# Six PSUM banks for the last weight-gradient products, two for the rows beside them

## The chip, the core and the metric

One kernel runs on one core of a Trainium2 chip. The metric is the device time of one execution in microseconds. The execution that the profiler recorded has a span of its own, from its first to its last recorded instruction, and a device time a little longer than that span.

## The reference, cut to what matters

A forward pass of two residual blocks and its full gradient. `x` is 2048 x 448; block A multiplies its two-dimensional spectrum by learned weights, block B is an MLP over the 2048 tokens (hidden size F = 1792).

```python
h   = x + irfft2(rfft2(layernorm(x)) * (w_r + 1j * w_i))
h2  = h + mlp(layernorm(h))                 # w1: 2048x1792, w2: 1792x2048, gelu between
out, vjp = jax.vjp(h2_of, x, w_r, w_i, w1, b1, w2, b2)
return out, *vjp(grad_out)                  # out_0 .. out_7
```

The end of the kernel makes three of the outputs. `out_6` is the gradient of `w2` (1792 x 2048) and `out_4` that of `w1` (2048 x 1792): products of two 2-D operands contracted over the 448 columns. `out_1` is the gradient of `x`: rows of an inverse transform, put through the backward of a layer norm.

## The kernel before, in words

All work of TensorE, VectorE, ScalarE and of SyncE's queue stands in the order in which the program emits it; GpSimd's order alone is left to the scheduler.

PSUM has eight banks. `ps_ff()` (L177) and `ps_mm()` (L180) each hand out tiles of 128 x 512 fp32, one bank each, from two rings of four.

**Background products.** `gw_gen` (L1279) is a generator that yields once per unit of work. It runs over `u`, pairs of 128-row blocks of a weight gradient, and over four column blocks `c` of up to 512 columns. The contraction of 448 is three whole steps of 128 and one of 64. For the two row blocks of a pair, the two 64-row steps sit in one stationary tile (rows 0 to 63 for `i = 0`, 64 to 127 for `i = 1`); `parts` issues them as a pair of 64-row matmuls into two banks. A column block is thus six whole matmuls (`whole`), one pair of 64-row matmuls (`parts`), and two copies out of PSUM (`out`, through `evac`). The generator takes column blocks two at a time: six wholes of the first, then one visit of 64-row matmuls for both, then the copies of the first and the six wholes of the second. That is 14 units (`yield`) for two column blocks, 7 each.

Two such generators are queued in `pending`: one for `out_6` (7 pairs `u`, 196 units), then one for `out_4` (8 pairs, 224 units, its last column block of each `u` 256 wide). `fill(n)` takes n units from them, and after each unit pops one entry of `row_ops`. `evac` (L190) gives a copy to ScalarE or VectorE by the running totals of `Meter`, a cost table in the program. `store` and `st_load` issue the stores and the transposed loads of later stationary tiles on SyncE.

**The inverse rows.** After `s2_stage` (L687), whose last round uses the four `ff` banks for the last time in that form, `inv_rows` (L751) walks 16 row tiles. With two `aT` buffers it runs one tile ahead. Tile t of the loop is, in order of the program: `first(t+1)` (four 128-column matmuls into an `ff` bank, copied to `rAT` by ScalarE), `fill(8)`, then `py` (four 224-column matmuls into the two halves of another `ff` bank), then `gx_consumer`.

`gx_consumer` (L1346) puts the row's work into `row_ops`, to be popped during the next tile's `fill(8)`:

- `scaled_sum`: ScalarE reads the lower half of `py`, with a row sum;
- `low` and `high`: VectorE reads the upper half of `py` twice, once forwards and once reversed; after `high` the bank is free;
- `products`: a VectorE product with a row sum, and two GpSimd operations on single columns;
- `line`, `add_line`, `finish`: three VectorE operations in SBUF, held back for two tiles.

Before the change the order popped is `scaled_sum`, `low`, `line`, `high`, `add_line`, `products`, `finish`, where `line`, `add_line` and `finish` are those of two tiles earlier. After the 16 tiles, `drain()` runs what is left of `pending`.

Units, counted from the loops: `rows` and the fill after it take 54, `s2_stage` takes 33 in each of five rounds, 13 of them ahead of its second group of small matmuls and 20 at the round's end. When the last round's `after` hook is reached, 199 units are gone: all 196 of the first generator and three wholes of the second. 44 more are taken before `inv_rows`, 128 in it, and 49 in `drain()`.

Of the kernel before, what the change touches and what calls it, by code (L numbers as in the profile page):

```python
# [11 lines left out]
F32 = mybir.dt.float32  # L12
# [5 lines left out]
P = 128  # L18
# [23 lines left out]
N_FILL_B = (16, 16, 30, 8, 24, 8)  # L42
# [61 lines left out]
class Ring:  # L104
# [7 lines left out]
    def next(self):  # L112
        v = self.views[self.i % len(self.views)]
        self.i += 1
        Ring.release(v)
        return v
# [8 lines left out]
def kernel(  # L125
# [32 lines left out]
    psum = ctx.enter_context(tc.tile_pool(name="psum", bufs=1, space=bass.MemoryType.PSUM))  # L158
# [15 lines left out]
        n = int(np.prod(dims))  # L174
        return Ring([cut(reg, off + i * n, *dims) for i in range(count)])

    def ps_ff(parts=P):  # L177
        return psum.tile([P, 512], F32, tag="ff", bufs=4, name="ps_ff")

    def ps_mm():  # L180
        return psum.tile([P, 512], F32, tag="mm", bufs=4, name="ps_mm")


    def evac(out, in_, scale=None):
        n = int(np.prod(in_.shape[1:]))
        if load[0] + sc.cost('copy', n, False) <= load[1] + ve.cost('tensor_copy', n, in_.dtype == BF16):
            if scale is None:
                sc.copy(out=out, in_=in_)
            else:
                sc.activation(out=out, in_=in_, func=ACT.Copy, scale=scale)  # L190
        elif scale is None:
            ve.tensor_copy(out=out, in_=in_)
        else:
            ve.tensor_scalar(out=out, in0=in_, scalar1=scale, scalar2=None, op0=ALU.mult)
# [9 lines left out]
    def defer(us, fn, *views):  # L204
        state = [fn]

        def run():
            if state:
                state.pop()()
        later.append((clock[0] + us, len(later), run))  # L210
        later.sort(key=lambda x: x[0])
        for v in views:
            Ring.held.setdefault(id(v), []).append(run)
# [5 lines left out]
    def mm(out, lhsT, rhs, start, stop):  # L219
        nc.tensor.matmul(out, lhsT=lhsT, rhs=rhs, start=start, stop=stop)  # L220
        clock[0] += int(np.prod(rhs.shape[1:])) / 2400.0
        run_due()
# [373 lines left out]
    X_ring = ring(rC, 0, 2, 4, 2, KW)  # L596
# [189 lines left out]
    pending, row_ops = [], []  # L786

    def fill(n):
        while n > 0 and pending:
            try:  # L790
                next(pending[0])
                n -= 1
                if row_ops:
                    row_ops.pop(0)()
            except StopIteration:
                pending.pop(0)
# [101 lines left out]
    for c in range(2):  # L898
        for e in range(2):
            sc.copy(out=Rp.rearrange("p (e a q b c) -> p c e a q b", e=2, c=2, q=8, a=2)[:, c, e],  # L900
                    in_=Rm[:, 64 * c + 32 * e:64 * c + 32 * e + 32].rearrange("p (q a b) -> p a q b", q=8, a=2))
# [161 lines left out]
    for jp in range(NFB // 2):  # L1063
# [7 lines left out]
        for jj, ta, tb in spans:  # L1071
            fb = f0 + jj
            pu = pus[jj]
            for t in range(ta, tb):
                mm(pu[:, 0:D], lhsT=w1c[:, t, jj * P:(jj + 1) * P], rhs=hln[:, t, :],
                                 start=(t == 0), stop=(t == NT - 1))
# [136 lines left out]
    def load_du(q):  # L1213
        n = du_t[q].shape[1] * 512
        nc.sync.dma_start_transpose(out=du_t[q].rearrange("p j b q -> p (j b) q"), in_=rD[:, 2048 * q:2048 * q + n])
# [8 lines left out]
    st_next = iter(st_at)  # L1224

    def st_load(n):
        if n < 15:
            reg, j = order[n]
            nc.sync.dma_start_transpose(out=st_at[n], in_=reg[:, j * 1024 + 64:j * 1024 + 960])
# [3 lines left out]
    def load_xall(q):  # L1233
        nc.sync.dma_start(out=xall[:, 4 * q:4 * q + 4, :], in_=x_pt[:, 4 * q:4 * q + 4, :])
# [38 lines left out]
    ost = ring(rO, 0, 6, S // 2)  # L1273
    o4 = out_4.rearrange("(p t) f -> p t f", t=NT)

    def gw_gen(n, rhs, width, store, ost, u0=0):
        for u in range(u0, u0 + n // 2):
            st = next(st_next)

            def whole(pw, w, c, i, k, start, stop):  # L1280
                mm(pw[i][:, 0:w], lhsT=st[:, 4 * i + k, :], rhs=rhs(c, k, 0, P), start=start, stop=stop)

            def parts(pw, w, c, start):
                for i in range(2):
                    mm(pw[i][:, 0:w], lhsT=st[64 * i:64 * i + 64, 3, :], rhs=rhs(c, 3, 64 * i, 64 * i + 64),
                       start=start, stop=not start)

            def out(pw, w, c, i):
                o = os_[i]
                x = c % 2 * 512  # L1290
                evac(out=o[:, x:x + w], in_=pw[i][:, 0:w])
                if x:
                    if c == 3 and i and u != 3:
                        st_load(u + 4 if u < 3 else u + 3)
                    defer(1.5, lambda j=2 * (u - u0) + i: store(j, 512 * (c - 1), x + w, o), o)

            for c in range(0, 4, 2):
                os_ = [ost.next(), ost.next()]
                pw = [ps_mm(), ps_mm()]
                for i in range(2):  # L1300
                    for k in range(3):
                        whole(pw, 512, c, i, k, k == 0, False)
                        yield
                w = min(512, width - 512 * (c + 1))
                pv = [ps_mm(), ps_mm()]
                parts(pw, 512, c, False)
                parts(pv, w, c + 1, True)
                for i in range(2):
                    out(pw, 512, c, i)
                yield  # L1310
                yield
                for i in range(2):
                    for k in range(3):
                        whole(pv, w, c + 1, i, k, False, k == 2)
                        if k == 2:
                            out(pv, w, c + 1, i)
                        yield

    def store_4(t, a, n, o):
# [8 lines left out]
    for t in range(NT - LAG, NT + 4):  # L1328
        if t == 13:
            st_load(3)  # L1330
        if t == NT - 2:
            fill(8)
        rows(t)
    fill(N_FILL_B[2])
    Meter.slack = 7.0
    s2_stage(lambda s: X_ring.next(), bwd_mult, 13, 20, N_FILL_B[4], {0: lambda: load_du(1), 1: lambda: (load_du(0), load_xall(0)), 2: lambda: load_xall(1), 3: lambda: load_du(2)},
             2.0 * INV_SD)
    Meter.slack = 2.0
    g_out = w_io(out_2, out_3, True)
# [3 lines left out]
    def gx_consumer(t, py):  # L1343
        if t in X_AT:
            load_xall(X_AT[t])
        for _ in range(GW_AT.count(t)):  # L1346
            next(g_out, None)
        pb, tmp = (r448[:, t % 8 * D:(t % 8 + 1) * D], r452[:, t % 8 * D:(t % 8 + 1) * D])
        ms, m1, m2 = (lcol[:, NT + t, k:k + 1] for k in range(3))
        u, s2, s1 = (gcol[:, t, k:k + 1] for k in range(3))  # L1350
        nmean, rstd2, md = (xcol[:, k, t:t + 1] for k in range(3))
        rstd, xt, h = rstd_x[:, t:t + 1], xall[:, t, :], D // 2

        def scaled_sum():
            sc.activation(out=tmp[:, 0:h], in_=py[:, 0:h], func=ACT.Identity, scale=rstd, accum_out=ms)
            gp_.tensor_scalar(out=m1, in0=ms, scalar1=-2.0 / D, scalar2=None, op0=ALU.mult)  # L1356
            gp_.tensor_scalar(out=u, in0=ms, scalar1=md, scalar2=None, op0=ALU.mult)

        def low():
            ve.scalar_tensor_tensor(out=pb[:, 0:h], in0=py[:, h:D], scalar=rstd, in1=tmp[:, 0:h],  # L1360
                                    op0=ALU.mult, op1=ALU.add)

        def high():
            ve.scalar_tensor_tensor(out=pb[:, h:D], in0=py[:, D - 1:h - 1:-1], scalar=nrstd_x[:, t:t + 1],
                                    in1=tmp[:, h - 1::-1], op0=ALU.mult, op1=ALU.add)

        def products():
            ve.tensor_tensor_reduce(out=tmp, in0=pb, in1=xt, scale=-1.0 / D, scalar=0.0,
                                    op0=ALU.mult, op1=ALU.add, accum_out=m2)
            gp_.tensor_scalar(out=s2, in0=m2, scalar1=u, scalar2=rstd2, op0=ALU.subtract, op1=ALU.mult)  # L1370
            gp_.tensor_scalar(out=s1, in0=s2, scalar1=nmean, scalar2=m1, op0=ALU.mult, op1=ALU.add)

        def line():
            ve.tensor_scalar(out=tmp, in0=xt, scalar1=s2, scalar2=s1, op0=ALU.mult, op1=ALU.add)

        def add_line():
            ve.tensor_tensor(out=pb, in0=pb, in1=tmp, op=ALU.add)

        def finish():
            ve.tensor_tensor(out=pb, in0=pb, in1=dh[:, t, :], op=ALU.add)  # L1380
            if t % 2:
                s = (t - 1) % 8
                defer(2.0, lambda: nc.sync.dma_start(
                    out=out_1[0].rearrange("(p t) d -> p t d", t=NT)[:, t - 1:t + 1, :], in_=cut(r448, s * D, 2, D)))

        now = [scaled_sum, low, high, products]
        row_ops.append(now.pop(0))
        old = held_ops.pop(0) if len(held_ops) == 2 else []
        while now or old:
            for ops in (now, old):  # L1390
                if ops:
                    row_ops.append(ops.pop(0))
        held_ops.append([line, add_line, finish])
# [41 lines left out]
```

## Time and profile before

| | |
|---|---|
| time, median of 3 runs | 344.67 us (344.52 to 345.07) |
| device time of the profiled execution | 345.03 us |
| its span | 343.3 us |
| granted TensorE clock, mean | 1.00 |
| TensorE busy | 329.5 us (96%) |
| VectorE busy | 250.8 us (73%) |
| ScalarE busy | 206.7 us (60%) |
| GpSimd busy | 73.7 us (21%) |

In the profile's lines PE is TensorE, PEld its loading of stationary tiles, DVE VectorE, ACT ScalarE, POOL GpSimd, SP SyncE. A row gives a start in us from the span's start and a duration; starts of one engine closer together than the durations mean that the work is pipelined. `L84`, `L220` and `L225` are the lines of helpers, so that operations are told apart by their tiles: `ps_ff` and `ps_mm` are the two rings, `csI,rAT` the operands of `py`, `RTm` that of `first`, `rst`, `rS` the stationary tiles of `gw_gen`.

### The profile page before, as it was taken

To read this page: it belongs to the slowest core of one execution; us is meant where nothing else is said; L and a number is where in the kernel's file an instruction comes from. 1 tells how busy PE (TensorE), PEld (TensorE's weight loads), DVE (VectorE), ACT (ScalarE), POOL (GpSimd) and SP (SyncE) were. 2 spreads that over 40 slices of the span, in tenths; PEclk is the share of its full clock that TensorE was granted. 3 is DMA by queue.
4 is the path that set the end of the run, shared out by engine and by line. 5 is a ranking of instruction groups with operands and counts; after the bars stand their busy time and mean duration, and the time that the engine had idled before them with its cause. 6 is when DMAs were issued, how large, how long until landed. Compare 5 with 4: busy or idle time off the path is not lost.

```text
span 343.3 us, 7935 instructions
## 1 busy us (share of the span) xinstructions
PE 329.5 (96%) x2868; PEld 173.6 (51%) x2877; DVE 250.8 (73%) x669; ACT 206.7 (60%) x447; POOL 73.7 (21%) x235
## 2 busy tenths in 40 slices
PE   8798979999999999999999999999999999999995
PEld 4475644456645555555555555554333334555552
DVE  8999438724966888594325988786589985599993
ACT  5987647856966553513221346565488875688882
POOL 7766202441220000001001111110000000156660
PEclk9999999999999999999999999999999999999999
DMA  7999999979899999767976988836898898999975
GB/s 265 397 171 179 173 262 174 185 144 253 242 346 307 333 278 253 177 204 221 207 179 137 169 190 180 169 96 186 223 288 236 214 262 244 295 238 295 231 289 203
DMA packets 138606, 78.03 MB, mean 227 GB/s; under 512 B 88072, under 2 KB 130440, under 8 KB 138440
## 3 DMA queue, kind: packets, MB, share of 16 engines
q1 hardware_dynamic: 137000, 75.28, 86.9%
q0 software_dynamic: 1280, 1.86, 3.0%
q8 instruction: 22, 0.36, 0.5%
q10 hardware_dynamic: 288, 0.39, 0.3%
q14 instruction: 16, 0.13, 0.1%
HBM read 27.81 MB, written 22.04 MB: 145 GB/s over the span
## 4 chain that ended last, share of the span: by engine, by line
PE 69%; DVE 2%; ACT 1%; issue 1%; POOL 0%; DVEq 0%; ACTq 0%
PE ps_mm L220 62%; PE ps_ff L220 6%; PE ps_ff L225 2%; DVE rA L84 1%; ACT rO L84 1%; DVE r L84 0%; ACT rC L84 0%; DVE rS L84 0%; DVE rO L84 0%; DVE rB L84 0%; POOL lcol L1183 0%; ACT rAT L84 0%; DVEq L1430 0%; ACT r L84 0%; ACT rstd_h L84 0%
## 5 line engine op out<-in xcount | busy, mean ns | idle before, releaser
L220 PEld LDWEIGHTS <-r 128*128 128x128 bf16 (+2 forms) x628 | 58.5, 105 | 47.3 <-issue 2.8
L220 PEld LDWEIGHTS <-rS 128*128 128x128 bf16 (+1 forms) x468 | 36.2, 97 | 34.9 <-issue 6.4
L84 ACT CAST rO<-ps_mm 128x512 bf16<-128x512 f32 (+1 forms) x70 | 37.3, 583 | 15.9 <-PE ps_mm L220 14.1
L220 PE MATMUL ps_mm<-rD,r 128*128 128x448 bf16 x224 | 44.5, 352 | 0.0
L220 PEld LDWEIGHTS <-rst 128*128 128x128 bf16 (+1 forms) x320 | 23.5, 97 | 31.4 <-issue 14.1
L220 PE MATMUL ps_mm<-rC,rE 128*128 128x448 bf16 x144 | 31.5, 353 | 0.9 <-ACT rE L84 0.9
L220 PE MATMUL ps_mm<-rB,r 128*128 128x448 bf16 x160 | 31.2, 352 | 0.1
L220 PE MATMUL ps_mm<-rG,rst 128*128 128x512 bf16 (+1 forms) x121 | 26.8, 380 | 1.1 <-issue 0.8
L220 PE MATMUL ps_mm<-r,rst 128*128 128x512 bf16 (+2 forms) x144 | 27.4, 345 | 0.0
L84 ACT CAST r<-ps_ff 128x452 bf16<-128x452 f32 x44 | 23.9, 586 | 5.2 <-PE ps_ff L225 3.0
L84 ACT ACTIVATE r<-ps_mm,rstd_h 128x448 bf16<-128x448 f32 x16 | 10.1, 634 | 26.8 <-PE ps_mm L220 26.8
L84 DVE SCALAR_TENSOR_TENSOR r<-ps_mm,b2col,r 128x448 bf16<-128x448 f32 x16 | 10.9, 682 | 19.9 <-PE ps_mm L220 18.2
L84 ACT ACTIVATE r<-rC 128x448 bf16<-128x448 bf16 x16 | 9.1, 571 | 26.7 <-DMA out_dram<-r 22.5
L1183 POOL TENSOR_SCALAR lcol<-lcol 128x1 f32<-128x1 f32 x16 | 8.5, 530 | 64.7 <-ACT r L84 64.7
L84 ACT ACTIVATE rG<-rG 128x896 bf16<-128x896 bf16 x14 | 13.3, 950 | 14.9 <-DVE rG L84 14.7
L220 PEld LDWEIGHTS <-rO 128*128 128x128 bf16 (+1 forms) x165 | 15.2, 98 | 12.0 <-ACT rO L84 0.2
L220 PE MATMUL ps_ff<-csI,rAT 113*128 113x224 bf16 (+1 forms) x108 | 19.0, 298 | 0.6 <-ACT rAT L84 0.4
L84 ACT CAST rS<-ps_ff 128x512 bf16<-128x512 f32 x31 | 18.0, 584 | 2.0 <-PE ps_ff L220 1.7
L1356 POOL TENSOR_SCALAR lcol<-lcol 128x1 f32<-128x1 f32 x16 | 3.7, 234 | 70.7 <-ACT r L84 69.6
L220 PE MATMUL ps_mm<-rC,rO 128*128 128x448 bf16 x80 | 18.5, 353 | 0.0
L220 PEld LDWEIGHTS <-rE 128*128 128x128 bf16 x144 | 13.0, 98 | 10.6 <-ACT rE L84 1.2
L84 DVE TENSOR_SCALAR rG<-rG 128x896 bf16<-128x896 bf16 x28 | 10.9, 389 | 10.0 <-ACT rG L84 10.0
(197 smaller groups left out, 639.6 us busy)
## 6 DMA issues: line engine op xcount, KB each, us to landing
out_dram<-rO SPq DMA_DIRECT2D x34, 256.0 KB
r<-in_B_w_dram SPq DMA_DIRECT2D x5, 1024.0 KB
r<-r SPq DMA_DIRECT2D x12, 226.0 KB
r<-in_B_w_dram SPq DMA_DIRECT2D x3, 896.0 KB
rS<-in_B_w_dram SPq DMA_DIRECT2D x3, 896.0 KB
out_dram<-rG SPq DMA_DIRECT2D x10, 256.0 KB
rB<-in_B_w_dram SPq DMA_DIRECT2D x4, 512.0 KB
rO<-in_B_w_dram SPq DMA_DIRECT2D x2, 1024.0 KB
```

Source lines behind the costliest of these rows:

```text
L84: fn(**kw)
L220: nc.tensor.matmul(out, lhsT=lhsT, rhs=rhs, start=start, stop=stop)
L225: nc.tensor.matmul(out, lhsT=lhsT, rhs=rhs, start=start, stop=stop)
L1183: gp_.tensor_scalar(out=m1, in0=ms, scalar1=-1.0 / D, scalar2=None, op0=ALU.mult)
L1356: gp_.tensor_scalar(out=m1, in0=ms, scalar1=-2.0 / D, scalar2=None, op0=ALU.mult)
```

## The change

The two rings become eight tiles made once and handed out in turn. `gw_gen` goes through a flat list of (u, c) and joins one column block with `joined[0]` later ones, also across pairs `u`: one, as before, until a new hook `join` in the last round of `s2_stage` sets it to two. The same hook moves two `ff` banks to the `mm` ring, which then has six, and leaves two for the rows. `gx_consumer` pops `scaled_sum`, `low` and `high` ahead of the older tile's work. An output buffer is taken when its first copy is emitted, and no longer when its column block is begun.

```diff
-    def ps_ff(parts=P):
-        return psum.tile([P, 512], F32, tag="ff", bufs=4, name="ps_ff")
+    ff_banks = Ring([psum.tile([P, 512], F32, name=f"ps_ff{i}") for i in range(4)])
+    mm_banks = Ring([psum.tile([P, 512], F32, name=f"ps_mm{i}") for i in range(4)])
+
+    def ps_ff():
+        return ff_banks.next()
 
     def ps_mm():
-        return psum.tile([P, 512], F32, tag="mm", bufs=4, name="ps_mm")
+        return mm_banks.next()
+
+    def turned(r):
+        k = r.i % len(r.views)
+        return r.views[k:] + r.views[:k]
...
+    joined = [1]
+
     def gw_gen(n, rhs, width, store, ost, u0=0):
...
+        pairs = [(u, c) for u in range(u0, u0 + n // 2) for c in range(4)]
+
+        def begin(u, c):
+            if u not in sts:
+                sts[u] = next(st_next)
+            return u, c, min(512, width - 512 * c), [ps_mm(), ps_mm()]
...
+        while pairs:
+            p = begin(*pairs.pop(0))
+            for i in range(2):
+                for k in range(3):
+                    whole(p, i, k, k == 0, False)
+                    yield
+            more = [begin(*pairs.pop(0)) for _ in range(min(joined[0], len(pairs)))]
+            parts(p, False)
+            for q in more:
+                parts(q, True)
+            for i in range(2):
+                out(p, i)
+            for _ in range(1 + len(more)):
+                yield
+            for q in more:
                 for i in range(2):
                     for k in range(3):
-                        whole(pv, w, c + 1, i, k, False, k == 2)
+                        whole(q, i, k, False, k == 2)
                         if k == 2:
-                            out(pv, w, c + 1, i)
+                            out(q, i)
                         yield
...
+    def join():
+        joined[0] = 2
+        free = turned(ff_banks)
+        mm_banks.views, mm_banks.i = free[:2] + turned(mm_banks), 0
+        ff_banks.views, ff_banks.i = free[2:], 0
+
     Meter.slack = 7.0
-    s2_stage(lambda s: X_ring.next(), bwd_mult, 13, 20, N_FILL_B[4], {0: lambda: load_du(1), 1: lambda: (load_du(0), load_xall(0)), 2: lambda: load_xall(1), 3: lambda: load_du(2)},
+    s2_stage(lambda s: X_ring.next(), bwd_mult, 13, 20, N_FILL_B[4], {0: lambda: load_du(1), 1: lambda: (load_du(0), load_xall(0)), 2: lambda: load_xall(1), 3: lambda: load_du(2), 4: join},
...
         now = [scaled_sum, low, high, products]
-        row_ops.append(now.pop(0))
+        for _ in range(3):
+            row_ops.append(now.pop(0))
         old = held_ops.pop(0) if len(held_ops) == 2 else []
```

More of the change, by code (lines that the diff above doesn't have):

```diff
@@ L1274, with whole, parts, out @@
     o4 = out_4.rearrange("(p t) f -> p t f", t=NT)
+    joined = [1]
     def gw_gen(n, rhs, width, store, ost, u0=0):
[L1277 to L1299, printed above, removed]
+        sts, outs = {}, {}
+        pairs = [(u, c) for u in range(u0, u0 + n // 2) for c in range(4)]
[3 more added lines that the diff above has]
+            return u, c, min(512, width - 512 * c), [ps_mm(), ps_mm()]
+        def whole(p, i, k, start, stop):
+            u, c, w, pw = p
+            mm(pw[i][:, 0:w], lhsT=sts[u][:, 4 * i + k, :], rhs=rhs(c, k, 0, P), start=start, stop=stop)
+        def parts(p, start):
+            u, c, w, pw = p
+            for i in range(2):
+                mm(pw[i][:, 0:w], lhsT=sts[u][64 * i:64 * i + 64, 3, :], rhs=rhs(c, 3, 64 * i, 64 * i + 64),
+                   start=start, stop=not start)
+        def out(p, i):
+            u, c, w, pw = p
+            if (u, c // 2) not in outs:
+                outs[u, c // 2] = [ost.next(), ost.next()]
+            o = outs[u, c // 2][i]
+            x = c % 2 * 512
+            evac(out=o[:, x:x + w], in_=pw[i][:, 0:w])
+            if x:
+                if c == 3 and i and u != 3:
+                    st_load(u + 4 if u < 3 else u + 3)
+                defer(1.5, lambda j=2 * (u - u0) + i: store(j, 512 * (c - 1), x + w, o), o)
+        while pairs:
[8 more added lines that the diff above has]
+                parts(q, True)
+            for i in range(2):
+                out(p, i)
+            for _ in range(1 + len(more)):
+                yield
+            for q in more:
@@ L1300, in gw_gen @@
                 for i in range(2):
                     for k in range(3):
[L1302 to L1313, printed above, removed]
-                        whole(pv, w, c + 1, i, k, False, k == 2)
+                        whole(q, i, k, False, k == 2)
```

## The prediction

> **What bounds the kernel now.** I read the page's forty slices first, then the table of stretches for the part that the change can reach (from 284 us on), then the timelines of PE, ACT and DVE there, row tile by row tile.
>
> ```profile
> PE   8798979999999999999999999999999999999995
> ...
> DVE  8999438724966888594325988786589985599993
> ACT  5987647856966553513221346565488875688882
> ...
> PEclk9999999999999999999999999999999999999999
> ```
>
> PE is full to the last slice, DVE nearly full in slices 35 to 38. The stretch of the row tiles:
>
> ```profile
> 294.00:330.00 36.00, 36.00 (x279) 20.86 (x278) 32.56 (x100) 29.98 (x79) 19.48 (x57) 1.00 1.04 273
> ```
>
> The columns after the window are PE, PEld, DVE, ACT and POOL busy, then the clock. PE never stops in these 36 us, DVE is busy for 90% of them. The list of waits names no wait of PE here: PE alone sets the pace, by the work it is given. So PE work removed here is worth its full length, and a PE wait added here costs its full length. How close such a wait is, one row tile shows:
>
> ```profile
> 298.28 0.56 PE L220 MATMUL ps_ff<-csI,rAT 113*128 113x224 bf16 x4
> 298.67 0.39 PE L220 MATMUL ps_ff<-RTm,r 128*113 128x128 bf16 x4
> ...
> 300.41 0.55 PE L220 MATMUL ps_ff<-csI,rAT 113*128 113x224 bf16 x4
> ```
> ```profile
> 299.15 0.59 ACT L84 CAST rAT<-ps_ff 113x512 bf16<-113x512 f32 x1
> 299.63 0.45 ACT L84 ACTIVATE r<-ps_ff,rstd_x 128x224 bf16<-128x224 f32 x1
> ```
> ```profile
> 300.21 0.45 DVE L84 SCALAR_TENSOR_TENSOR r<-ps_ff,rstd_x,r 128x224 bf16<-128x224 f32 x1 [1.18 <-ACT r L84]
> 300.58 0.44 DVE L84 SCALAR_TENSOR_TENSOR r<-ps_ff,nmr_h,r 128x224 bf16<-128x224 f32 x1
> ```
>
> This is the second row tile. `py` starts at 298.28, `first` follows at 298.67, ScalarE copies that (299.15) before it comes to `scaled_sum` (299.63), `low` starts at 300.21, `high` at 300.58, and `high` ends at 301.02. That is 2.74 us after `py` began, with DVE idle for 1.18 us beforehand, so it is the bare chain without a queue. The next `py` started at 300.41, 0.61 us before that end. It could, since there are four banks.
>
> **The part with a saving: fewer visits.** The joining starts after 199 units, three wholes into the second generator, so its 32 column blocks are all that changes. Two to a visit make 16 visits, three to a visit 11 (ten of three, one of two): 5 fewer. The matmuls stay the same in number. What a visit costs by itself:
>
> ```profile
> 328.65 0.70 PE L220 MATMUL ps_mm<-r,rst 128*128 128x512 bf16 x3
> 329.19 0.38 PE L220 MATMUL ps_mm<-rC,rst 64*128 64x512 bf16 x2
> 329.50 0.56 PE L220 MATMUL ps_ff<-csI,rAT 113*128 113x224 bf16 x4
> ```
> ```profile
> 328.95 0.12 PEld L220 LDWEIGHTS <-rst 64*128 64x128 bf16 x4 [0.42 <-issue]
> ```
>
> The last whole starts at 328.65; the first 64-row pair begins with its loads at 328.95, 0.30 to 0.31 later; the second pair starts at 329.19, `py` 0.31 after it. Wholes follow each other at 0.216. So a visit costs 0.095 on the way in and as much on the way out, 0.19 together, and 5 visits are 0.95 us. By their place: 3 visits become 2 before the row tiles, 10 become 7 between them, 3 become 2 in `drain()`. The 0.19 before and the 0.19 after are on the path whatever the rows do; the other 0.57 count only if PE does not wait there.
>
> **The part with a price: rows on two banks.** `first(0)` takes bank A, `first(1)` bank B, `py(0)` A, and from there each `first` takes B and each `py` A, until at the end there is no `first(16)` and `py(15)` takes B. So `py(1)` to `py(14)` must each wait for the `high` of the tile before: 14 new waits. `first` waits for nothing new: its bank was copied a whole tile earlier. The chain from `py` to `py`, from the rows above: 1.35 to `scaled_sum`, 0.58 to `low`, 0.37 to `high`, 0.44 for `high`, and 0.05 until PE starts (the chain of waits shows 0.04 to 0.05 between an ACT or DVE end and the PE instruction it releases). Sum 2.79 us. The new order of `row_ops` is in this already: the rows are of a tile with no `line` between `low` and `high`; with it `high` comes 0.30 later. Popping three entries does not speed up the 1.35, which is the `first` matmuls, their copy to `rAT`, and ScalarE's order.
>
> Now the pace of before, from `py(0)` to `py(14)`:
>
> ```profile
> 295.63 0.55 PE L220 MATMUL ps_ff<-csI,rAT 113*128 113x224 bf16 x4
> ```
> ```profile
> 327.06 0.55 PE L220 MATMUL ps_ff<-csI,rAT 113*128 113x224 bf16 x4
> ```
>
> 31.43 us for 14 tiles, 2.245 each. The chain takes 14 x 2.79 = 39.06. To that come tiles in which ScalarE has a copy of a finished product ahead of `scaled_sum`. That is so when the first unit of a `fill(8)` ends a column block. Before, one tile shows it plainly:
>
> ```profile
> 311.34 0.55 PE L220 MATMUL ps_ff<-csI,rAT 113*128 113x224 bf16 x4
> ```
> ```profile
> 313.16 0.51 ACT L84 ACTIVATE r<-ps_ff,rstd_x 128x224 bf16<-128x224 f32 x1
> ```
>
> 1.82 in place of 1.35. With 21 units to a round of three column blocks, copies fall after units 7 (two), 12, 15, 18 and 21 of a round; the first unit of `fill(8)` meets one for rows 5, 7, 8 and 11 (row 14's `high` is waited for by none). At 0.48 each (ScalarE starts copies of 512 columns 0.48 apart), about 1.9 us; nearly all copies there were on ScalarE before, and a copy on VectorE at that point would fit into its idle time and cost nothing. So 0 to 1.9, and I take 1.9.
>
> Row stage: 39.06 + 1.9 - 31.43 = 9.5 us more. It hides the three visits saved between the rows. Behind the waiting `py` on PE's queue stand the next `first`, eight units and their copies, so everything is late with it; nothing else in the stretch can use the time. With the two outer visits: 9.5 - 0.4 = 9.1 us. On the profiled execution (345.03, 0.36 above the median of the runs) that is 354.1, on the median 353.8. I forecast **353.8 us**.
>
> **A bound from below on the wait.** `low` and `high` read the upper half of the bank, and the first two `py` matmuls write the lower. If only the third matmul waited, 0.19 us after the first (four start within 0.39), the cycle would be 2.60: 14 x 2.60 + 1.9 - 31.43 - 0.4 = 6.5 us, so 351.2. No row shows matmuls writing one half of a bank while another engine reads the other; every reader here takes a finished bank. I stay with 2.79. The Trainium skill's "PSUM — Partial Sum Buffer", section "PSUM bank collisions raise a hardware error", says that two engines may not touch one bank in the same partitions at once even at different columns, which would rule the 2.60 out; no run here shows it yet.
>
> **DVE's new order** matters only if it fills the cycle. The three operations of the older tile now follow each other directly and each needs the one before:
>
> ```profile
> 333.64 0.38 DVE L84 TENSOR_SCALAR r<-rE,stats 128x448 bf16<-128x448 bf16 x1
> 334.06 0.39 DVE L84 TENSOR_TENSOR r<-r,r 128x448 bf16<-128x448 bf16 x1
> 334.49 0.42 DVE L84 TENSOR_TENSOR r<-r,rA 128x448 bf16<-128x448 bf16 x1
> ```
>
> 0.42 and 0.43 apart, where alternating they start 0.30 apart. A tile then takes 0.37 + 0.48 + 0.55 + 0.42 + 0.43 + 0.30 = 2.55 of DVE, against 2.18 before; below 2.79, so hidden by the wait on the bank. Without that wait it would itself cost up to 0.3 a tile.
>
> **Edits with no cost of their own.** Tiles made once in place of a tagged ring, and the flat list, give the same order of banks and instructions up to the hook; if a hazard is tracked differently it could be some tenths either way. Taking an output buffer later lets a store go out a few units later on SyncE's queue; ring buffers and the 1.5 us delay cover it. Stationary tiles across pairs are read at most one visit earlier, two pairs after their load was issued (over 10 us). PE's clock stays: the stretch from 228.5 to 232.5 us has 0.65 us without PE at a clock of 1.00, and the new waits are about that long.
>
> **Rivals.**
>
> A, faster: the waits do not come about or hide, and five visits are saved: 343.7. Its condition is a `high` that ends within 2.2 us of its `py`; the bare chain is 2.74, and ScalarE's part comes before any edited line. Weak.
>
> B, the half bank: 351.2, as above.
>
> C, DVE becomes the bound: each tile gets a copy of 0.56 from `Meter` on top of 2.55, so 3.1: 14 x 3.1 - 31.43 - 0.4 = 11.6, that is 356.3. It decides from a copy in every second tile (0.24 of slack). Against it: before, VectorE got copies in the first four tiles alone.
>
> D, nothing measurable happens, within 0.2% (0.7 us, about what a measurement of this kernel can tell from no change): it needs waits of 1 us in sum.
>
> **How the numbers follow.** Forecast 0.72, B 0.13, C 0.09, A 0.04, D 0.02. Faster by over 0.2% 0.04, within 0.02, slower 0.94. The range runs from B without the ScalarE delays (349.3, taken to 349.0) to C with a little more (356.8). A and D lie outside it.
>
> **What would show it.** In the profile after: `py` starts 2.75 to 2.85 apart, PE waiting some 0.5 us for DVE ahead of each `py` but the first and last, PE busy near 80% in the row stage, `high` before `line`; 11 visits of 64-row loads after 284 us, not 16; DVE idle time for ScalarE ahead of `low`. If `py` starts before the `high` of the tile before has ended, the half-bank case holds; if PE has no wait on DVE there, I am wrong altogether.

## The result, and the profile after

| | before | after |
|---|---|---|
| median | 344.6 us (4 runs, 344.31 to 345.07) | 354.75 us (4 runs, 353.85 to 357.25) |
| device time of the profiled execution | 345.03 | 354.25 |
| its span | 343.3 | 352.4 |

The ratio is 1.0305, with a 95% interval of 1.025 to 1.036: 10 us slower, where 353.8 us was forecast. A ratio, here and below, is taken over the fast runs alone, without executions in a slower state that the chip shows at times, so it can differ a little from the quotient of the medians.

The slices of the page show the place at once. The engine's name is followed by its busy share in tenths, 40 slices of the span:

```profile
PE   8879999999999999999999999999999999877795
...
DVE  8989558707938887772248888775998854888894
```

PE, full to the end before, falls to 7 and 8 tenths in slices 35 to 38, and DVE has idle time there too. The stretch from the first `py` to the 15th, as one row of the table of stretches (PE, PEld, DVE, ACT, POOL busy, clock, DMA share, GB/s):

```profile
294.90:336.40 41.50, 32.94 (x243) 17.84 (x240) 34.08 (x93) 27.57 (x72) 18.54 (x54) 1.00 0.75 225
```

The same rows before:

```profile
295.60:327.10 31.50, 31.50 (x243) 18.34 (x242) 29.12 (x91) 26.39 (x70) 17.62 (x51) 1.00 1.03 267
```

PE has 243 matmuls in both, and is busy for 79% of the longer stretch. The clock stayed at 1.00. The list of waits, for PE from 284 us on, names a waiter that the list of before did not have (the waiting engine, the one waited for, then total, times, longest):

```profile
PE ps_ff L227 <- DVE r L84: 8.1, 11, 1.1
```

And one row tile in the timeline, the counterpart of the one in the prediction, by engine:

```profile
297.75 0.56 PE L227 MATMUL ps_ff<-csI,rAT 113*128 113x224 bf16 x4 [0.50 <-DVE r L84]
...
298.15 0.39 PE L227 MATMUL ps_ff<-RTm,r 128*113 128x128 bf16 x4
...
298.63 0.58 ACT L84 CAST rAT<-ps_ff 113x512 bf16<-113x512 f32 x1 [0.76 <-PE ps_ff L227]
...
299.11 0.45 ACT L84 ACTIVATE r<-ps_ff,rstd_x 128x224 bf16<-128x224 f32 x1
...
299.69 0.45 DVE L84 SCALAR_TENSOR_TENSOR r<-ps_ff,rstd_x,r 128x224 bf16<-128x224 f32 x1 [1.32 <-ACT r L84]
...
300.05 0.44 DVE L84 SCALAR_TENSOR_TENSOR r<-ps_ff,nmr_h,r 128x224 bf16<-128x224 f32 x1
...
300.55 0.56 PE L227 MATMUL ps_ff<-csI,rAT 113*128 113x224 bf16 x4
```

Read it as a chain: `py` 297.75, copy of `first` 298.63, `scaled_sum` 299.11, `low` 299.69, `high` 300.05 to 300.49, next `py` 300.55. That is 2.80 us, and the next `py` starts 0.06 after `high`. It does so after every one of rows 0 to 13; only `py(15)`, which has the other bank, is free.

Where the 10 us lie, from PE's starts in the two profiled executions:

| stretch | before | after | difference |
|---|---|---|---|
| start to the last 32-row matmul of `s2_stage` | 284.29 | 283.30 | -0.99 |
| from there to `first(0)` | 9.59 | 9.80 | +0.21 |
| `first(0)` to `py(0)` | 1.75 | 1.87 | +0.12 |
| `py(0)` to `py(14)` | 31.43 | 41.43 | +10.00 |
| `py(14)` to `py(15)` | 2.44 | 2.65 | +0.21 |
| `py(15)` to the last matmul | 9.79 | 9.36 | -0.43 |
| last matmul to the end | 3.96 | 4.03 | +0.07 |

The first row lies ahead of the hook, in code that only hands its banks out differently. In the later runs of kernels with the very same code there, that point fell between 283.3 and 287.6 us, so the -0.99 is the scatter of one execution.

The work of PE in `py(0)` to `py(14)`, the row stage from here on, can be split by the distances between its starts: each matmul's own (0.216 us for 512 columns), the extra 0.094 at each step between whole and 64-row matmuls, and what is left, which I call stalls. Before: 16 such steps, 1.51 us, no stalls. After: 10 steps, 0.95 us, and 10.65 us of stalls. The list of waits shows less, 8.1 us, because a row of 512 columns is drawn 0.38 us long although the next can start after 0.216; the list counts from the end of that row.

### The profile page after: what moved, and what is told of

The parts are those of the page before. It is cut to its first block, busy times and chain, and to the rows that moved or that the text cites. A ratio compares the mean times of both kernels' runs of the same rounds, so it can differ in the third digit from the quotient of the medians.

```text
span 352.4 us, 7956 instructions
## 1 busy us (share of the span) xinstructions
PE 331.0 (94%) x2868; PEld 173.5 (49%) x2877; DVE 255.4 (72%) x668; ACT 207.8 (59%) x448; POOL 73.0 (21%) x235
## 4 chain that ended last, share of the span: by engine, by line
PE 60%; ACT 4%; DVE 3%; issue 3%; DMA 3%; SPq 1%; POOL 0%; ACTq 0%; DVEq 0%
PE ps_mm L227 51%; PE ps_ff L227 8%; DVE r L84 2%; PE ps_ff L232 2%; ACT r L84 1%; DMA out_dram<-rW 1%; ACT rO L84 1%; ACT rG L84 1%; DMA rst<-rB 1%; DMA out_dram<-rG 1%; DVE rA L84 1%; ACT rAT L84 1%; SPq L1340 0%; ACT rC L84 0%; DVE rS L84 0%
## 5 line engine op out<-in xcount | busy, mean ns | idle before, releaser
L84 ACT CAST rO<-ps_mm 128x512 bf16<-128x512 f32 (+1 forms) x63 | 33.7, 577 | 15.9 <-PE ps_mm L227 14.0
L84 ACT CAST rAT<-ps_ff 113x512 bf16<-113x512 f32 x24 | 13.8, 585 | 14.3 <-PE ps_ff L227 14.3
L227 PE MATMUL ps_mm<-r,rst 128*128 128x512 bf16 (+3 forms) x96 | 19.7, 354 | 0.0
```

What stands on the lines that cost most here:

```text
L84: fn(**kw)
```

## The experiments

Theory: `py` waits in its one bank for the `high` of the row before, through the chain of 2.80 us. Rivals: the tiles made once (a hazard followed differently), the joined visits (copies in bunches), and the new order on VectorE. Each kernel below was compared with the kernel before on the chip that both ran on; there the kernel before took 343.6 to 352.6 us in single runs, so times differing by less than about 1 us are settled here by the traces.

**No hook, old order: tiles made once and the flat list alone.**

```diff
-    s2_stage(lambda s: X_ring.next(), bwd_mult, 13, 20, N_FILL_B[4], {0: lambda: load_du(1), 1: lambda: (load_du(0), load_xall(0)), 2: lambda: load_xall(1), 3: lambda: load_du(2), 4: join},
+    s2_stage(lambda s: X_ring.next(), bwd_mult, 13, 20, N_FILL_B[4], {0: lambda: load_du(1), 1: lambda: (load_du(0), load_xall(0)), 2: lambda: load_xall(1), 3: lambda: load_du(2)},
...
-        for _ in range(3):
-            row_ops.append(now.pop(0))
+        row_ops.append(now.pop(0))
```

> The changed kernel without the hook and with the old order of the row operations: the tiles made once, the flat list and the later taking of output buffers stay. Bank theory: as before, 344.3 to 345.0 us. Rival that a hazard is followed differently on tiles made once: part of the 9 us is here, over 347 us.

345.41 us against 346.67, ratio 0.998 (0.995 to 1.001). In the trace `py(0)` to `py(14)` took 31.43 us again, without stalls. These edits cost nothing.

**Two column blocks to a visit, the rest as changed.**

```diff
-        joined[0] = 2
+        joined[0] = 1
```

> The changed kernel with two column blocks to a visit after the hook, as before it; six and two banks and the new order stay. Bank theory (py waits on its own bank for the high of the tile before): the row stage keeps its 2.80 us from py to py, and only the two visits outside it come back, 0.4 us, so 355 us. Rival that the joined visits of three do the harm (their six copies bunch up): 345 to 347 us and py again 2.25 apart.

353.0 us against 346.67, ratio 1.021 (1.016 to 1.027); span 350.5. The wait stays without the joining, so the joining is not the cause. But I expected this kernel to be 0.4 us slower than the changed one, and its row stage is 1.87 us shorter (39.56 for 41.43). The same tile, row 5, in both: here `py` to `py` is 2.80, in the changed kernel 3.29 (309.19 to 312.48).

```profile
308.80 0.56 PE L227 MATMUL ps_ff<-csI,rAT 113*128 113x224 bf16 x4
...
311.60 0.56 PE L227 MATMUL ps_ff<-csI,rAT 113*128 113x224 bf16 x4 [0.29 <-DVE r L84]
```

With 14 units to a round the copies fall elsewhere against `fill(8)`. Only row 7 has one ahead of `scaled_sum`; with 21 units rows 5, 7, 8 and 11 have. Row 7 of the changed kernel shows it on ScalarE, two copies of a finished product before the `ACTIVATE`:

```profile
315.28 0.56 PE L227 MATMUL ps_ff<-csI,rAT 113*128 113x224 bf16 x4 [0.93 <-DVE r L84]
...
316.15 0.59 ACT L84 CAST rAT<-ps_ff 113x512 bf16<-113x512 f32 x1 [1.30 <-PE ps_ff L227]
...
316.63 0.66 ACT L84 CAST rG<-ps_mm 128x256 bf16<-128x256 f32 x2
...
317.16 0.47 ACT L84 ACTIVATE r<-ps_ff,rstd_x 128x224 bf16<-128x224 f32 x1
```

So once the rows set the pace, joining three blocks saves 0.56 us of steps there and costs 2.6 us of stalls (10.65 against 8.05).

**Six and two banks with the old order.** The second edit of the first experiment alone, on the changed kernel.

> The changed kernel with the old order of the row operations (line of the older tile between low and high). Bank theory: the chain is longer by the 0.30 us of line, so 3.10 from py to py, 14 x 0.30 = 4.2 us more than the changed kernel, 358 to 359 us. Rival that VectorE's new order is the bound: its 2.55 us a tile fall back to 2.18, so faster than the changed kernel, 346 to 349 us.

358.42 us, ratio 1.036 (1.031 to 1.041); span 356.4, 4.0 over the changed kernel's. `line` stands between `low` and `high` again:

```profile
309.25 0.45 DVE L84 SCALAR_TENSOR_TENSOR r<-ps_ff,rstd_x,r 128x224 bf16<-128x224 f32 x1 [0.85 <-ACT r L84]
309.62 0.39 DVE L84 TENSOR_SCALAR r<-rE,stats 128x448 bf16<-128x448 bf16 x1
309.92 0.44 DVE L84 SCALAR_TENSOR_TENSOR r<-ps_ff,nmr_h,r 128x224 bf16<-128x224 f32 x1
```

`py` is 3.10 apart (307.32 to 310.42), as expected, although VectorE has less to do per tile. That the whole stage is 4.0 longer, near the 14 x 0.30 expected, is partly chance: rows 0 and 1 have no older `line` and stay at 2.80, and row 2, with a VectorE copy between `line` and `high`, takes 3.71. This speaks against VectorE as the bound of the changed kernel: DVE waits 0.85 us for ScalarE here.

**The kernel before with the new order alone.**

```diff
-        row_ops.append(now.pop(0))
+        for _ in range(3):
+            row_ops.append(now.pop(0))
```

> The kernel before with one edit: scaled_sum, low and high are popped ahead of the older tile's operations; four and four banks, visits of two. Bank theory: VectorE needs 2.55 us a tile instead of 2.18 and falls back by 0.3 a tile; py shares a bank with the py two tiles before, which gives 1.7 us of slack, used up after some six tiles, so 0 to 2.5 us more, 344.6 to 347.1. Rival that the order alone is the cause: 352 us or more, py 2.8 apart.

350.46 us against 346.67, ratio 1.013 (1.008 to 1.017); span 348.0. The price is real and larger than I said. VectorE needs 2.57 us a tile:

```profile
318.51 0.44 DVE L84 SCALAR_TENSOR_TENSOR r<-ps_ff,rstd_x,r 128x224 bf16<-128x224 f32 x1
...
319.90 0.39 DVE L84 TENSOR_SCALAR r<-rE,stats 128x448 bf16<-128x448 bf16 x1
320.33 0.41 DVE L84 TENSOR_TENSOR r<-r,r 128x448 bf16<-128x448 bf16 x1
320.77 0.39 DVE L84 TENSOR_TENSOR r<-r,rA 128x448 bf16<-128x448 bf16 x1
321.08 0.44 DVE L84 SCALAR_TENSOR_TENSOR r<-ps_ff,rstd_x,r 128x224 bf16<-128x224 f32 x1
```

`line`, `add_line`, `finish` start 0.43 and 0.44 apart, each needing the result of the one before. PE was not held: `py(0)` to `py(14)` took 31.43 us. VectorE fell back tile by tile, its last `high` ended 41.3 us after `py(0)`, 4.4 later than in the kernel before (36.9), and the debt came due at the end, where the last copies out of PSUM queue behind the rows. My limit on how far it could fall back was wrong: `py(14)` started at 327.46, before the `high` of row 12 ended at 329.60, so the tagged tiles of before do not go round strictly in turn as I had taken them to. In the changed kernel this order costs nothing, since 2.57 lies inside 2.80.

**`scaled_sum` ahead of the copy to `rAT` (e5).**

```diff
+            if halves_:
+                fill(1)
             if s1 + ahead_ < NT:
                 q.append(first(s1 + ahead_))
             aT = q.pop(0)
-            fill(n_fill)
+            fill(n_fill - 1 if halves_ else n_fill)
```

> The changed kernel with first(t+1) put behind the first unit of fill(8), so that scaled_sum no longer stands behind the copy to rAT on ScalarE. Bank theory: the chain loses 0.49 us (1.35 becomes about 0.86, as row 15 shows, where there is no copy) and would be 2.30; then VectorE's 2.57 us a tile in the new order is the next bound, so 2.57 to 2.60 from py to py, 3 us less than the changed kernel. If the wait were for something else than that chain, py would stay 2.80 apart.

350.41 us against 345.47, ratio 1.015 (1.011 to 1.019). The row stage took 36.48 us, 2.605 a tile. That this lies at the 2.57 to 2.60 expected is partly chance, since it is a mean of unlike rows: six take 2.57 or 2.58, rows 5, 7, 8 and 11, with a copy ahead of `scaled_sum`, 2.74 to 2.79, row 3 3.05, and rows 0 to 2 2.03 to 2.66. It is 4.95 less than in the changed kernel, not the 3 expected: the chain lost more than 0.49, for `scaled_sum` starts 0.59 to 0.63 after `py` where no copy is ahead of it, and not 0.86, and the rows with a copy became shorter too. In the six rows `scaled_sum` comes first on ScalarE, and what ends last is VectorE's own queue: `low` starts 0.31 after `finish`, as in the experiment before it.

```profile
320.69 0.45 ACT L84 ACTIVATE r<-ps_ff,rstd_x 128x224 bf16<-128x224 f32 x1
321.04 0.19 ACT L84 ACTIVATION_READ_ACCUMULATOR r<-ps_ff,rstd_x 128x1 f32 x1
321.19 0.59 ACT L84 CAST rAT<-ps_ff 113x512 bf16<-113x512 f32 x1
```
```profile
321.50 0.39 DVE L84 TENSOR_TENSOR r<-r,rA 128x448 bf16<-128x448 bf16 x1
321.81 0.44 DVE L84 SCALAR_TENSOR_TENSOR r<-ps_ff,rstd_x,r 128x224 bf16<-128x224 f32 x1
```

**The same, with `line` popped ahead of `products`.**

```diff
         old = held_ops.pop(0) if len(held_ops) == 2 else []
+        if old:
+            row_ops.append(old.pop(0))
```

> As e5, and the older tile's line is popped ahead of products, so that the three dependent VectorE operations no longer follow each other directly: 0.37 + 0.36 + 0.30 + 0.55 + 0.42 + 0.30 = 2.30 us of VectorE a tile. Bank theory with VectorE as the second bound: 2.30 to 2.40 from py to py, some 346 us where the kernel before has 344.6. If the order of VectorE does not matter, as in e5.

349.97 us, ratio 1.012 (1.007 to 1.016); 35.05 us of row stage, 2.50 a tile. The order of VectorE matters, by 0.10 a tile, but 2.30 to 2.40 is missed. The reason is in how I put it: a tile takes the longer of the chain and PE's own work, and both vary. The five tiles with a visit of three took 2.44 to 2.79, rows 5, 8 and 11 with a copy ahead of `scaled_sum` 2.73 to 2.74, row 3 with VectorE late 2.90, the other five 2.03 to 2.33. The mean of the longer ones lies above both means.

**Two banks by turns (e6).** `first(t+1)` and `py(t)` share a bank and the next tile takes the other, so that a row has two tiles' time for `high`. Old order.

```diff
-        def first(s1):
-            pa = ps_ff()
+        def first(s1, pa=None):
+            pa = ps_ff() if pa is None else pa
...
+            bank = ps_ff() if halves_ else None
+            n_ahead = 1 if halves_ else 0
+            fill(n_ahead)
             if s1 + ahead_ < NT:
-                q.append(first(s1 + ahead_))
+                q.append(first(s1 + ahead_, bank))
             aT = q.pop(0)
-            fill(n_fill)
-            py = ps_ff()
+            fill(n_fill - n_ahead)
+            py = bank if halves_ else ps_ff()
```

> Six and two banks and visits of three as in the changed kernel, but first(t+1) and py(t) share a bank, the two banks by turns, so that py has two tiles' time for its high; first stands behind the first unit of fill(8); old order of the row operations. Bank theory: no wait for high is left; py waits at most for the copy to rAT, some 0.4 us in the four tiles with a copy of a product ahead of it; the saved visits (0.95) pay for part of that: 0 to 1 us more than before. If two banks were too few in any order, 350 us or more.

345.72 us against 345.47, ratio 1.0005 (0.997 to 1.004). Row stage 31.93 us, stalls 1.26. The list of waits for PE from 284 us on, where the changed kernel has 8.1 us:

```profile
PE ps_ff L227 <- DVE r L84: 0.2, 1, 0.2
```

The whole loss is gone with the same two banks, so it was not their number. In 13 of the 14 rows `py` now started before the `high` of the row before had ended, by up to 0.92 us, which one bank for every `py` did not allow. Turns alone were not run: this kernel also moves `first`, which without turns (e5) took away half of the loss, and the next one moves `scaled_sum` instead.

**The same, `first` ahead of `fill(8)` and `scaled_sum` at once (e9).**

```diff
-            n_ahead = 1 if halves_ else 0
+            n_ahead = 0 if halves_ else 0
...
-        row_ops.append(now.pop(0))
+        now.pop(0)()
```

> As e6, but first stands ahead of fill(8) again and scaled_sum is emitted at once behind py, so that on ScalarE it comes ahead of the copy to rAT and of every copy of a product. Bank theory: scaled_sum starts 0.86 us after py, high ends within 2.6, the bank's next writer comes 2.6 us after py, so no PE wait over 0.1 us, and the five saved visits show: 0.5 to 1.0 us less than before. If the fall of 0.95 us is not there although PE does not wait, the visit's price is wrong.

345.86 us, ratio 1.002 (0.999 to 1.005). Four stalls add to 1.31 us; three, of 0.62, 0.29 and 0.29, are of `first`, whose bank is held by a `high` that VectorE does late. So no gain was seen: the steps saved 0.57 us between the rows, the stalls took 1.31.

**`first` behind one unit, and behind two (e11).**

```diff
-            n_ahead = 0 if halves_ else 0
+            n_ahead = 1 if halves_ else 0
```

In the second kernel the 1 is a 2.

> As e9, with first behind the first unit of fill(8). In e9 PE stood 1.3 us in the row stage, nearly all of it first waiting for the high of two rows earlier, up to 0.62 us. Bank theory: first comes 0.22 us later, so the stalls fall to some 0.6 us, the ten transitions into and out of visits cost 0.95 where before they cost 1.51, and the whole is level with before or 0.3 us below. If the stalls do not shrink with the place of first, they are not the bank's.

> As e9, with first behind the second unit of fill(8). Bank theory: first waits for next to nothing; py, which shares its bank, may now wait for the copy to rAT where a copy of a product is ahead of it on ScalarE: stalls 0.2 to 0.8 us, total 0.2 to 0.7 us below before. If two banks cannot carry the rows at the old pace, the stalls stay over 1 us in another place.

With one unit: 345.76 us against 346.19, ratio 1.0005 (0.998 to 1.003), row stage 31.31 us, stalls 0.64: the stalls halve as expected, and the stretch is 0.12 shorter than before. The table of stretches shows PE at rest for 0.24 us of it:

```profile
296.20:327.50 31.30, 31.06 (x242) 19.05 (x240) 29.53 (x92) 27.29 (x71) 19.44 (x52) 1.00 1.02 256
```

With two: 347.28 us, ratio 1.005 (1.001 to 1.008), row stage 32.03 us, stalls 1.38, of which 0.83 are of `py`, now behind the copy to `rAT`; more than I allowed for, and over the 1 us in another place that I had named as the sign against two banks. With `first` this late they do not carry the rows at the old pace; with `first` one unit earlier they do. The list of waits for PE from 284 us on names it:

```profile
PE ps_ff L227 <- DMA out_dram<-rG: 1.1, 1, 1.1
PE ps_ff L227 <- ACT rAT L84: 0.6, 2, 0.3
PE ps_ff L227 <- DVE r L84: 0.3, 1, 0.3
```

The first of these is a wait of `first(0)`, ahead of the rows, and no part of the stalls counted here.

**The last one with visits of two.** The edit of the second experiment on it.

> As e11, with visits of two column blocks to the end. Visit theory: five more visits, 0.95 us over e11 where the stalls are the same; ScalarE's copies fall elsewhere against the rows, which can move the stalls by 0.5 us either way. If visits cost nothing, e11 and this are equal.

348.11 us, ratio 1.006 (1.004 to 1.009), 0.83 over the kernel with visits of three, too little for the medians to settle. In the row stage (33.75 us for 32.03) 16 steps cost 1.50 us instead of 0.94, and the stalls rose from 1.38 to 2.37. The steps are as priced; the stalls moved more than the 0.5 I gave them. No version was measurably faster than the kernel before.

## Why the prediction was right, step by step

**What bounds the kernel.** That PE had no slack in the row stage held: stalls of 10.65 us there came out as 10.0 us of time.

**The visit.** 0.095 for each step into or out of a visit was forecast, 0.094 measured. The five visits did go away (16 to 11). Their outer part did not show as forecast, 0.4 us less: the stretches around the rows add up to 0.2 more. Two parts of that are visits of three lying where one of two lay (0.12 and 0.21, about a pair of 64-row matmuls; one such pair is missing from the last stretch). Another 0.38 us is `first(0)` standing, a wait that the prediction did not have. Three later kernels with the same instructions there did not have it either: 9.42 for 9.80, and 9.59 before, so there the 0.19 shows. What it waits for stays open. The profile names a store of `rG`, but in the program `first(0)` uses no output buffer; its operand `D3` is written by transfers `r<-r`, which the profile names for the same instruction in e5 (1.5 us).

**The chain.** 2.79 forecast, 2.80 measured, in every row without a copy in the way. The bare chain was read off one tile of before in which VectorE happened to be idle; that is what made it right.

**Copies ahead of `scaled_sum`.** 1.9 us forecast. Measured: 41.43 - 14 x 2.80 = 2.2, of which rows 5, 7, 8 and 11 have 0.48 to 0.54 each, as named. The missing 0.24 is row 3, where VectorE does a product's copy of 0.68 ahead of `low`; the prediction had such a copy fit into VectorE's idle time and cost nothing.

**The half bank.** `py` starts 0.06 after `high` in all 14 rows, although its first two matmuls write the half that `high` does not read. The 2.60 is out. The wait stands in the program; whether the chip would bear a matmul in one half while VectorE reads the other, which the Trainium skill's "PSUM — Partial Sum Buffer", section "PSUM bank collisions raise a hardware error", rules out, was not tried.

**VectorE's new order.** 2.55 forecast, 2.57 measured, and hidden, as the two experiments with it show. Rival C did not come about: after row 2, `Meter` gave VectorE no copies in the row stage. No row shows its term of 0.56 for such a copy; a copy of 512 columns held VectorE for 0.60 (303.21 to 303.81 in row 2).

**Edits with no cost.** Without the hook and the new order they had none: the row stage took 31.43 us, as before. That the tagged tiles give the same order of banks as a ring is another matter: the kernel before with the new order speaks against it (`py(14)` started before the `high` of row 12 had ended).

**The size.** The row stage was forecast 9.5 longer and was 10.0; the outer saving of 0.4 did not come. So 10.15 in the medians in place of 9.1. The sign of "some 0.5 us" of waiting ahead of each `py` was too low even by the forecast's own terms, which give (9.5 + 0.57) / 14 = 0.72; measured were 0.14 to 1.23, 0.76 on average.

## What to carry to other kernels

Before taking PSUM banks away from a stage, measure the life of each tile in it, from its first matmul to the end of its last reader, in a tile where the readers' engines were idle; a tile that outlives the stage's period needs a second bank, or its turns must be arranged so that the next writer of the bank comes a whole period later. Here the same two banks cost 10 us or nothing: 10 when every `py` had the same one, nothing when the calls shared them by turns and `first` came one unit later. And when a stage of fixed pitch runs beside a generator of another pitch, changing the generator's round moves its copies against the chain: check which rows have one ahead of the first link.

## What the runs showed of the hardware that was not expected

An order on VectorE alone, with the same instructions, moved a tile from 2.18 to 2.57 us: bf16 operations on 448 elements (0.38 to 0.39 long) start 0.30 apart when the next does not need the last one's result, and 0.42 to 0.45 apart when it does. Two such pairs come with the new order, and `products` now starts 0.47 after the `high` that it needs, where it came 0.36 after another operation. The debt did not slow TensorE at all while it grew and still cost 4 us, at the end.

Otherwise the runs agree with what the rows of before had shown: 0.094 us for each step between whole and 64-row matmuls, in visits of two and of three alike.
